# Issuing the transfers of v and of the weights from GpSimd's queue in an attention and gated-convolution kernel

## The chip, the cores and the metric

One core of a Trainium2 chip runs the program. The metric is the device time of one execution in microseconds (us), taken as the median of three runs. Engines are named as in the profile: PE (TensorE, with PEld for its weight loads), DVE (VectorE), ACT (ScalarE), POOL (GpSimd) and SP (SyncE). SPq is SP's queue, in which it issues transfers. Lnnn is a line of the kernel.

## The reference

Attention with a soft cap over 8 batches, 12 heads, 448 positions and a head size of 64, in float32, and behind it a gated feed-forward block:

```
scores = cap * tanh((q @ k.T / sqrt(64)) / cap)
attn   = exp(scores - max);  attn = attn / (sum(attn) + 1e-9)
x      = attn @ v, heads side by side      # (8, 448, 768)
gate   = sigmoid(conv over 5 positions of x with conv_w)
out    = (gate * (x @ w_val)) @ w_out
```

w_val and w_out are 768 x 768. They reach the kernel as 64-bit floats, and the kernel takes each apart into a high and a low part of 32 bits.

## The kernel before

Two heads of a batch make a pair; there are 48 pairs, and two pairs make a quad. For each pair the kernel loads q and k (`load_blocks`, L364: four transfers each, 56 KB apiece, in runs of 128 bytes), turns them by a transpose on DVE (`turn`, L515), multiplies q with k on PE (L542, and L553 for the remainder of 64 positions), and takes tanh and exp on ACT (L558, L562). Column sums (L610, into the tile `psz`) and the product with v (L636, into `psa` and `psz`) follow on PE, then a division and a convolution on DVE (L690), the product with w_val (L706 to L708), the gate, and the product with w_out (L741 to L743). The result goes out through `store` (ACT copies) and `store_out` (L754, a transfer from SP).

`load_v` brings v of a pair in three transfers: two of the tile `vn` (L377, 96 KB each) and one of `vh` (L378). `vn` and `vh` have two buffers each, and both pairs of a quad are read by all of its products with v, so that v of the next quad is loaded when these products have ended.

The weights come in twelve pieces, n = 0 to 5 of w_val and 6 to 11 of w_out, of 768 KB each. `weight_load(n)` (L451) brings piece n into `w_raw`, of which there is one buffer. Its conversion has three steps. The first reads `w_raw`: on DVE for pieces 0 to 3 (L306 to L309), on ACT for pieces 4 to 11 (L311, L312). The second is on DVE (L315, L316); L316 is the last to read `w_raw`, so piece n+1 can be loaded when L316 of piece n has ended. The third (L319 to L323, DVE) needs a copy of the piece that begins two bytes further on. For pieces 4 to 11 that copy is a second transfer of the same piece (`late_load`, L462, into the single buffer `w_late`), issued when the third step of the piece before has ended.

The tile `qkn` of q and k has one buffer through the first sixteen pairs, so q and k of a pair are loaded after `turn` of the pair before.

The order of the instructions on each engine is fixed: tables (PAIR, QUAD, BATCH, ONCE) give each step a due time in units of one pair, all steps are sorted by it, and each engine gets its instructions in that order. Every engine then works through its own list, and an instruction that waits holds up all that stand behind it on its queue. Before the change nearly all transfers stand in SP's list; ACT issues four at the very start, and POOL's list holds only seven memsets.

Of the kernel before, what the change touches and what calls it, by code (L numbers as in the profile page):

```python
# [20 lines left out]
P = 128  # L21
# [306 lines left out]
def quad_rows(w, g):  # L328

    return w[g * 2 * P:(g + 1) * 2 * P].rearrange("(p t) n -> p t n", t=2)  # L330
# [39 lines left out]
def load_v(nc, vn, vh, v, p):  # L370

    _, H, S, D = v.shape
    b, hp = divmod(p, H // 2)
    n = S // P * P
    r = p % 2 * (S - n)
    for j in range(2):
        nc.sync.dma_start(vn[:, j], v[b, 2 * hp + j, :n].rearrange("(t r) d -> r t d", r=P))  # L377
    nc.sync.dma_start(vh[r:r + S - n], v[b, 2 * hp:2 * hp + 2, n:].rearrange("j r d -> r j d"))  # L378


def fast_path(tc, io, u0, q, k, v, w_val, conv_w, w_out, out, capt):

    nc = tc.nc
    B, H, S, D = q.shape
# [14 lines left out]
    with ExitStack() as ctx:  # L399
# [48 lines left out]
        def weight_load(n):  # L448
            w, g, nh, _ = wsteps[n]
            wraw[n] = wsc.tile([P, 2, NH, 2], I32, name="w_raw")  # L450
            nc.sync.dma_start(  # L451
                wraw[n].rearrange("p t n two -> p t (n two)"), quad_rows(w.bitcast(I32), g)[:, :, nh * DM:(nh + 1) * DM]
            )

        def late_tile():
            return wsc.tile([P, 2, 4 * NH + 2], U16, name="w_late")

        def late_load(n):
            if n in BY_DMA:
                w, g, nh, _ = wsteps[n]  # L460
                wlate[n] = late_tile()
                nc.sync.dma_start(  # L462
                    wlate[n][:, :, 1:1 + 4 * NH], quad_rows(w.bitcast(U16), g)[:, :, nh * 2 * DM:(nh + 1) * 2 * DM]
                )

# [40 lines left out]
        def load_vp(p):  # L506
            if p % 2 == 0:
                vhalf[p // 2] = io.tile([P, 2, D], F32, name="vh")
            vloads[p] = io.tile([P, 2, NT, D], F32, name="vn")
            load_v(nc, vloads[p], vhalf[p // 2], v, p)  # L510
# [258 lines left out]
        def put(table, steps, count, unit, col):  # L769
# [16 lines left out]
        ), B, NPAIR, batch_column)  # L786
        steps = dict(
            weight_load=weight_load, late_load=late_load, val_first=val_first, weight_first=weight_first, weight_second=weight_second, weight_third=weight_third,
            free_scratch=free_scratch, free_pre=free_pre, cw_load=cw_load, cw_split=cw_split,
        )  # L790
# [179 lines left out]
```

## Time and profile before

| | |
|---|---|
| median of three runs | 689.23 us (688.55 to 689.86) |
| span of the profiled execution, first to last instruction | 686.2 us |
| PE busy | 659.0 us (96%) |
| DVE busy | 557.2 us (81%) |
| ACT busy | 499.7 us (73%) |
| POOL busy | 0.4 us |
| mean granted clock of TensorE | 0.992 |
| transfers issued by SP for v | 96 of `vn`, 48 of `vh` |
| transfers issued by SP for weights | 12 of `w_raw`, 8 of `w_late` |

No total time of the profiled execution is shown beside its span; the median of the runs stands 3.0 us above the span. A share of busy time is a mean over stages: the kernel first fills its pipeline and converts the weights, and then repeats one pattern for most of its time.

### The profile page before, as it was taken

How to read it: one execution, taken by the hardware profiler on the slowest of the kernel's cores; microseconds unless marked ns; L12 is line 12 of the kernel's file. 1: busy time of each engine (PE TensorE's matmuls, PEld its weight loads, DVE VectorE, ACT ScalarE, POOL GpSimd, SP SyncE). 2: the span in 40 equal slices, each digit the busy share in tenths (PEclk: the TensorE clock that was granted, in tenths of full speed). 3: DMA queues.
4: the chain of work that ended last, by engine and by line, in shares of the span. 5: the costliest groups of instructions: out<-in, count | busy, mean ns of one | idle time of the engine just before them, and what ended most of it. 6: DMA issues, size and time to landing. Idle time of an engine off the chain costs nothing.

```text
span 686.2 us, 11781 instructions
## 1 busy us (share of the span) xinstructions
PE 659.0 (96%) x4680; PEld 465.9 (68%) x4680; DVE 557.2 (81%) x776; ACT 499.7 (73%) x535; POOL 0.4 (0%) x7
## 2 busy tenths in 40 slices
PE   4787999999999999999999999999999999999996
PEld 1221484487596686786686696866766877767996
DVE  3899999989978889987979877988879896897530
ACT  5589769889684898777797695886788785975110
POOL 0000000000000000000000000000000000000000
PEclk9899999999999999999999999999999999999999
DMA  6769888423343432341334430433234432111001
GB/s 115 167 162 219 226 224 237 95 64 62 81 90 68 91 68 60 69 99 20 68 78 91 100 68 17 104 62 64 52 60 109 86 76 37 50 39 60 0 25 72
DMA packets 235165, 60.65 MB, mean 88 GB/s; under 512 B 226400, under 2 KB 226400, under 8 KB 235104
## 3 DMA queue, kind: packets, MB, share of 16 engines
q1 hardware_dynamic: 233248, 59.61, 39.2%
q8 instruction: 38, 0.62, 0.4%
q10 hardware_dynamic: 1856, 0.23, 0.3%
q14 instruction: 23, 0.19, 0.1%
HBM read 48.79 MB, written 11.01 MB: 87 GB/s over the span
## 4 chain that ended last, share of the span: by engine, by line
PE 86%; DVE 6%; SPq 3%; DMA 2%; issue 1%; ACT 1%; DVEq 0%; ACTq 0%
PE pss L542 13%; PE psa L636 10%; PE pss L706 9%; PE pss L708 8%; PE pss L707 8%; PE pss L741 8%; PE psz L636 8%; PE pss L743 7%; PE pss L742 7%; PE psz L610 4%; PE pss L553 3%; SPq L364 2%; DVE qkt L515 1%; DVE gate L690 1%; DMA qkn<-in_k_dram 1%
## 5 line engine op out<-in xcount | busy, mean ns | idle before, releaser
L558 ACT ACTIVATE pt<-pss,rc 128x896 f32<-128x896 f32 x144 | 139.8, 1003 | 69.6 <-PE pss L542 44.3
L562 ACT ACTIVATE pt<-pt,capt 128x896 f32<-128x896 f32 x144 | 145.5, 1041 | 0.6
L690 DVE SCALAR_TENSOR_TENSOR gate<-u,cw,gate 128x448 f32<-128x448 f32 x192 | 125.9, 674 | 1.7
L741 PE MATMUL pss<-wo,g_h 128*128 128x384 f32 x336 | 114.9, 342 | 0.0
L743 PE MATMUL pss<-wo,g_l 128*128 128x384 f32 x336 | 113.8, 339 | 0.0
L742 PE MATMUL pss<-wo,g_h 128*128 128x384 f32 x336 | 113.6, 338 | 0.0
L706 PE MATMUL pss<-xh,wv 128*128 128x448 f32 x288 | 105.8, 367 | 0.0
L707 PE MATMUL pss<-xh,wv 128*128 128x448 f32 x288 | 104.3, 362 | 0.0
L708 PE MATMUL pss<-xl,wv 128*128 128x448 f32 x288 | 104.3, 362 | 0.0
L741 PEld LDWEIGHTS pss<-wo,g_h 128*128 128x128 f32 x336 | 63.1, 188 | 9.3 <-ACT pt L558 5.7
L636 PE MATMUL psa<-pt,vn 128*32 128x448 f32 x576 | 69.1, 547 | 0.0
L636 PE MATMUL psz<-pt,vn 128*32 128x448 f32 x576 | 64.9, 541 | 0.7 <-DVE zt L641 0.7
L750 ACT COPY osb<-pss 128x768 f32<-128x768 f32 x28 | 22.3, 797 | 57.8 <-PE pss L743 56.8
L743 PEld LDWEIGHTS pss<-wo,g_l 128*128 128x128 f32 x336 | 63.1, 188 | 0.6 <-DVE g_l L425 0.6
L742 PEld LDWEIGHTS pss<-wo,g_h 128*128 128x128 f32 x336 | 63.1, 188 | 0.3 <-DVE wo L323 0.3
L706 PEld LDWEIGHTS pss<-xh,wv 128*128 128x128 f32 x288 | 54.0, 187 | 13.0 <-ACT pt L558 5.3
L515 DVE STREAM_TRANSPOSE qkt<-qkn 128x896 f32<-128x896 f32 x47 | 51.6, 1103 | 7.0 <-DMA qkn<-in_k_dram 3.5
L708 PEld LDWEIGHTS pss<-xl,wv 128*128 128x128 f32 x288 | 54.0, 188 | 3.6
L707 PEld LDWEIGHTS pss<-xh,wv 128*128 128x128 f32 x288 | 54.0, 188 | 3.5
L542 PE MATMUL pss<-qkt 64*128 64x448 f32 x144 | 37.5, 636 | 19.4 <-DVE guard L434 8.1
L586 DVE TENSOR_TENSOR pa<-pt 128x896 f32<-128x896 f32 x42 | 45.3, 1078 | 8.1 <-ACT pt L562 8.1
L718 DVE TENSOR_TENSOR gate<-pss,gate 128x896 f32<-128x896 f32 x24 | 26.1, 1088 | 31.1 <-PE pss L708 31.1
(86 smaller groups left out, 930.6 us busy)
## 6 DMA issues: line engine op xcount, KB each, us to landing
out_dram<-osb SPq DMA_DIRECT2D x28, 384.0 KB, 2.6
qkn<-in_q_dram SPq DMA_DIRECT2D x188, 56.0 KB, 2.3
qkn<-in_k_dram SPq DMA_DIRECT2D x188, 56.0 KB, 2.3
vn<-in_v_dram SPq DMA_DIRECT2D x96, 96.0 KB, 2.5
w_raw<-in_moe_w_val_dram SPq DMA_DIRECT2D x6, 768.0 KB, 4.8
w_raw<-in_moe_w_out_dram SPq DMA_DIRECT2D x6, 768.0 KB, 4.9
w_late<-in_moe_w_out_dram SPq DMA_DIRECT2D x6, 768.0 KB, 5.0
vh<-in_v_dram SPq DMA_DIRECT2D x48, 32.0 KB, 2.3
```

Source lines behind the costliest of these rows:

```text
L515: nc.vector.transpose(t.rearrange("p j s -> p (j s)"), loads.pop(p).rearrange("p j s -> p (j s)"))
L542: nc.tensor.matmul(ps[:, j, :S], st[x][r, 1, c], st[y][r, 0], start=(n == 0), stop=(n == len(parts) - 1))
L558: nc.scalar.activation(st["p", i], st.pop(("s", i)), AF.Tanh, scale=rc8)
L562: nc.scalar.activation(t, t, AF.Exp, scale=capt)
L636: nc.tensor.matmul(o, w, x, start=(q["n", t] == 1), stop=(q["n", t] == NT + 1))
L690: nc.vector.scalar_tensor_tensor(g, u, cw[:, i, c:c + 1], g, ALU.mult, ALU.add)
L706: nc.tensor.matmul(o[:, t, :S], w_h, xh, start=(c == 0), stop=False)
L707: nc.tensor.matmul(o[:, t, :S], w_l, xh, start=False, stop=False)
L708: nc.tensor.matmul(o[:, t, :S], w_h, xl, start=False, stop=(c == NCC - 1))
L741: nc.tensor.matmul(o[:, nh, :NH], g_h[:, d, s], w_h, start=(d == 0), stop=False)
L742: nc.tensor.matmul(o[:, nh, :NH], g_h[:, d, s], w_l, start=False, stop=False)
L743: nc.tensor.matmul(o[:, nh, :NH], g_l[:, d, s], w_h, start=False, stop=(d == NCC - 1))
```

## The change

144 transfers of v and 20 of the weights are issued from GpSimd's queue instead of SyncE's. The due times stay, so the moved transfers keep their order among themselves, and those that stay on SP keep theirs. Transfers of q, k, the convolution's weights and the output are as before, as are all buffers and all compute instructions.

```
@@ load_v
     for j in range(2):
-        nc.sync.dma_start(vn[:, j], v[b, 2 * hp + j, :n].rearrange("(t r) d -> r t d", r=P))
-    nc.sync.dma_start(vh[r:r + S - n], v[b, 2 * hp:2 * hp + 2, n:].rearrange("j r d -> r j d"))
+        nc.gpsimd.dma_start(vn[:, j], v[b, 2 * hp + j, :n].rearrange("(t r) d -> r t d", r=P))
+    nc.gpsimd.dma_start(vh[r:r + S - n], v[b, 2 * hp:2 * hp + 2, n:].rearrange("j r d -> r j d"))
@@ weight_load
-            nc.sync.dma_start(
+            nc.gpsimd.dma_start(
                 wraw[n].rearrange("p t n two -> p t (n two)"), quad_rows(w.bitcast(I32), g)[:, :, nh * DM:(nh + 1) * DM]
             )
@@ late_load
-                nc.sync.dma_start(
+                nc.gpsimd.dma_start(
                     wlate[n][:, :, 1:1 + 4 * NH], quad_rows(w.bitcast(U16), g)[:, :, nh * 2 * DM:(nh + 1) * 2 * DM]
                 )
```

## Rows read from the trace of the kernel before

**Rows 1.** The page's first part: busy time (share of the span) and instructions.

```profile
PE 659.0 (96%) x4680; PEld 465.9 (68%) x4680; DVE 557.2 (81%) x776; ACT 499.7 (73%) x535; POOL 0.4 (0%) x7
```

**Rows 2.** Busy time in stretches: PE, PEld, DVE, ACT, POOL, clock, DMA share, GB/s.

```profile
20.00:25.00 5.00, 3.36 (x12) 1.34 (x16) 4.23 (x13) 3.55 (x6) 0.00 (x0) 0.50 1.00 266
...
100.00:120.00 20.00, 20.00 (x149) 8.94 (x146) 18.87 (x27) 17.86 (x20) 0.00 (x0) 1.00 0.88 240
...
400.00:450.00 50.00, 50.00 (x347) 38.97 (x349) 40.95 (x55) 37.63 (x42) 0.00 (x0) 1.00 0.27 56
```

**Rows 3.** Waits of the compute engines, 78 to 140 us: total, times, longest.

```profile
PEld pss L742 <- DVE wo L323: 0.3, 1, 0.3
```

**Rows 4.** PE's timeline: start, length, instruction, idle before it and its releaser.

```profile
21.64 3.36 PE L542 MATMUL pss<-qkt 64*128 64x448 f32 x8 [5.48 <-DVE cw_m L306]
...
122.19 0.45 PE L742 MATMUL pss<-wo,g_h 128*128 128x384 f32 x1
```

**Rows 5.** DVE's timeline, the first 30 us.

```profile
10.99 1.11 DVE L515 STREAM_TRANSPOSE qkt<-qkn 128x896 f32<-128x896 f32 x1 [2.90 <-DMA qkn<-in_k_dram]
14.62 0.96 DVE L306 COPY w_late<-w_raw 128x1536 uint16<-128x1536 uint16 x1 [2.52 <-DMA w_raw<-in_moe_w_val_dram]
...
20.39 1.10 DVE L515 STREAM_TRANSPOSE qkt<-qkn 128x896 f32<-128x896 f32 x1
...
28.92 0.65 DVE L641 STREAM_TRANSPOSE zt<-psz 128x448 f32<-128x448 f32 x1 [1.69 <-PE psz L610]
```

**Rows 6.** SP's timeline, the first 20 us.

```profile
9.34 0.67 SPq L451 DMA_DIRECT2D w_raw<-in_moe_w_val_dram  x1
...
12.89 3.01 SPq L364 DMA_DIRECT2D qkn<-in_q_dram  x4
```

**Rows 7.** The chain that ended last, in order of time: start, length, what.

```profile
17.51 2.23 DMA qkn<-in_k_dram
```

**Rows 8.** ACT's timeline, conversion of the pieces 4, 8 and 9.

```profile
52.47 1.63 ACT L311 ACTIVATE w_t<-w_raw 128x768 f32<-128x768 f32 x1 [4.14 <-DMA w_raw<-in_moe_w_val_dram]
...
92.42 0.94 ACT L312 ACTIVATE w_raw<-w_raw 128x768 f32<-128x768 f32 x1
...
100.74 0.97 ACT L312 ACTIVATE w_raw<-w_raw 128x768 f32<-128x768 f32 x1
```

**Rows 9.** DVE's timeline, conversion of the pieces 4, 5, 8, 9 and 10.

```profile
55.52 0.96 DVE L316 TENSOR_TENSOR wv<-w_t,w_raw 128x768 fp32r<-128x768 f32 x1 [0.67 <-ACT w_raw L312]
...
69.17 0.56 DVE L319 TENSOR_SCALAR w_late<-w_late 128x768 int32<-128x768 int32 x1
...
93.53 0.96 DVE L316 TENSOR_TENSOR wo<-w_t,w_raw 128x768 fp32r<-128x768 f32 x1
...
101.77 0.96 DVE L316 TENSOR_TENSOR wo<-w_t,w_raw 128x768 fp32r<-128x768 f32 x1
...
110.70 0.96 DVE L316 TENSOR_TENSOR wo<-w_t,w_raw 128x768 fp32r<-128x768 f32 x1 [0.40 <-ACT w_raw L312]
```

**Rows 10.** SP's timeline, 60 to 90 us.

```profile
61.55 0.58 SPq L462 DMA_DIRECT2D w_late<-in_moe_w_val_dram  x1
...
80.74 0.55 SPq L462 DMA_DIRECT2D w_late<-in_moe_w_out_dram  x1
...
86.71 0.57 SPq L451 DMA_DIRECT2D w_raw<-in_moe_w_out_dram  x1
```

**Rows 11.** The tile w_raw: from issue to landing, shortest, median, longest.

```profile
DMA to landing us min/median/max: 4.6/4.9/5.9
```

**Rows 12.** The tile w_late: the same.

```profile
DMA to landing us min/median/max: 4.6/5.2/6.2
```

**Rows 13.** Issues of the tiles vn and qkn: ns shortest/median/longest, first and last start.

```profile
L377 SPq DMA_DIRECT2D vn<-in_v_dram x96: 368/487/1390, 19.1 to 624.0; - x96
...
L364 SPq DMA_DIRECT2D qkn<-in_q_dram x188: 311/477/1892, 5.3 to 567.9; - x188
```

**Rows 14.** Waits of SP's queue over the whole span: total, times, longest.

```profile
SPq L377 <- PE psa L636: 53.1, 4, 20.7
```

## Prediction

> **What bounds the kernel now.** I read the page's busy times first: PE works for 659.0 of a span of 686.2 us [rows 1], so about 27 us are all that any change of the queues could win. The view by stretches says where they lie. From some 80 us on PE is busy without a gap: 20.00 of 20 us at 100 to 120, 50.00 of 50 at 400 to 450, at full clock [rows 2]. In this long part a transfer that is issued earlier wins nothing, because PE has no gap to close. The gaps are at the start, where PE waits once for 5.48 us, and the clock stands at 0.50 (its lower level, 1.2 GHz) behind that gap, from 20 to 25 us [rows 2, 4].
>
> The second thing to see is that another engine stands just behind PE until the weights are converted. DVE is busy for 18.87 of the 20 us from 100 to 120 [rows 2], and at 122.19 us the product with w_out has to wait for DVE's last conversion step [rows 3, 4]. The wait is only 0.3 us, but it says that the conversion of the weights has no slack at its end. After it PE runs without gaps to the end, so whatever moves that point moves the end by as much. Thus the start must be followed along DVE, from the first turn to the last piece of w_out.
>
> Third I read, along this DVE line, which steps wait for a transfer. Each piece is loaded when L316 of the piece before has ended, is changed by ACT for nearly 2 us, and then comes back to DVE. In the pieces 8 and 9 ACT's L312 ends at 93.36 and 101.71, and DVE's L316 starts at 93.53 and 101.77 [rows 8, 9]: gaps of 0.17 and 0.06 us. In pieces 4 and 10 DVE already waits for ACT, by 0.67 and 0.40 us [rows 9], and in piece 4 ACT has waited 4.14 us for the transfer [rows 8]. The other late pieces (6, 7, 11) have wider gaps, and piece 5 waits on its second copy instead. So the latency of the w_raw transfer, median 4.9 us [rows 11], stands on the path in four of twelve pieces.
>
> **The change part by part.** The change takes 164 issues from SP and gives them to POOL, which has nothing else to do [rows 1]. Three effects follow.
>
> *a) The first piece is loaded earlier (gain).* On SP it is issued at 9.34, behind q and k of pair 1 [rows 6]; on DVE its conversion waits 2.52 us for it, until 14.62, though the turn of pair 1 has ended at 12.10 [rows 5]. POOL can issue it some 4 us earlier. Then DVE could convert from 12.10 on, and, at the 5.77 us that it takes (14.62 to 20.39), reach the turn of pair 2 at 17.9. That turn also needs k of pair 2, whose last transfer lands at 17.51 + 2.23 = 19.74 [rows 7]. Its loads start on SP at 12.89 and can start 0.71 us earlier without the issue of w_raw; the four of q took 3.01 us, where four medians make 1.9 [rows 6, 13], so up to 1.1 more if that came from the weight's transfer. k would land at 17.9 to 19.0, and the turn starts 1.4 to 2.5 us earlier. Against that, the weight's transfer now runs beside q and k of pair 1, and the first turn may slip. I take a gain of 1.3 us, with ends 0 and 2.5. It carries on, since PE's gap before 21.64 ends with this turn and DVE's next idle time, 1.69 us, is a wait for PE [rows 4, 5].
>
> *b) The same transfers from POOL take longer (loss).* The trace holds no transfer issued from POOL. Let c be the time that POOL's queue needs for one, where SP needs 0.49 for vn and 0.57 for w_raw [rows 10, 13]. From below it is bounded by SP's time; from above by the longest single issue in the trace, 1.89 us [rows 13]. I take twice SP's time of a weight, c = 1.1: nearer to the ordinary rows than to one outlier. Let what a landing takes longer be d = c - 0.55 = 0.55 us, if a transfer moves only once it is issued; the spread of the landings of w_raw, -0.3 to +1.0 about its median [rows 11], bounds d too. Then d falls on the path in pieces 4 and 10 in full (0.55 each), in piece 8 by 0.55 - 0.17 = 0.38, and in piece 9 by 0.55 - 0.06 = 0.49. Together 2.0 us. Pieces 1 to 3 and 5 to 7 and 11 hide it under DVE's other work; without that cover each would cost another 0.55.
>
> The Trainium skill (DMA: Bandwidth & Descriptors, Specifications) gives the first byte as about 1 us for GpSimd's path and 0.6 for SP's and ACT's; no run here shows it yet. By that figure d would be 0.4 (an estimate), this sum 0.4 + 0.4 + 0.23 + 0.34 = 1.4, and, with nothing under (c), the change would come out level.
>
> *c) POOL's queue falls behind where v stands ahead of a weight (loss).* The order of due times puts six transfers of v (two pairs) behind a transfer of weights and ahead of the next, at two places on the path. First: the second copy of piece 7 is issued at 80.74, six of v follow, and piece 8 at 86.71 [rows 10], when its buffer comes free. On POOL seven issues take 7.7 us, so that piece 8 leaves at 88.44: 1.7 us late, and piece 8 has no gap left under (b). Second: piece 5 is free to go when L316 of piece 4 ends, at 56.48 [rows 9]; with the six of v behind it POOL reaches the second copy of piece 5 at 56.48 + 7.7 = 64.2, where SP issued it at 61.55 [rows 10]. It lands 5.2 + 0.55 later [rows 12], at 69.9; DVE wants it at 69.17 [rows 9]. That is 0.8 us. Below c = 0.85 the first cost is nothing, below 1.0 the second.
>
> *d) q and k no longer stand behind v and the weights on SP (hidden).* v waits for its buffer on SP for up to 20.7 us at a time [rows 14], and what follows it waits too. This goes away, but those places lie in the part where PE has no gap [rows 2], and v on POOL has the whole time between the products of two quads. I cost it at nothing; the cover is PE's own work. The rule in the Trainium skill (DMA: Bandwidth & Descriptors, Issuing engines are not separate DMA queues) that issuing from several engines saves only the issue time agrees with the rows on PE.
>
> **The sum.** 2.0 + 1.7 + 0.8 - 1.3 = +3.2 us on the span, 686.2 to 689.4. The runs stand 3.0 us above the span, which I leave as it is: 689.23 + 3.2 = 692.4 us.
>
> **The rivals.**
>
> *Level.* If c is near 0.85, d is 0.3, (c) costs nothing and (b) is 0.3 + 0.13 + 0.24 + 0.3 = 1.0 us, against a gain of 1.3: 689 us. For it speaks that SP's issues are all near half a microsecond; against it that nothing in the trace ties POOL's time to SP's.
>
> *Faster.* The earlier turn of pair 2 shortens PE's gap before 21.64 so far that the clock does not fall. The eight matmuls there take 3.36 us at clock 0.50 [rows 2, 4]; at the full clock half, a gain of 1.7, and DVE's wait of 1.69 us for PE [rows 5] could use it. With POOL as quick as SP, 1.3 + 1.7 = 3.0 us: 686.2. This needs d below some 0.3 and a gap clearly shorter than 5.48 us. Against it: by my sum the gap still is over 4 us.
>
> *Much slower.* POOL's issues are held up by DVE, which is busy 18.87 of 20 us [rows 2], by one short conversion step of 0.56 us each time [rows 9]. Then c is some 1.6 and d about 1.0: (b) is 1.0 + 1.0 + 0.83 + 0.94 = 3.8, (c) 11.2 - 5.97 = 5.2 and 56.48 + 11.2 + 6.2 - 69.17 = 4.7, less 1.3: +12.4, 701.6 us. The Trainium skill (SBUF — State Buffer, Who interferes with whom) says that GpSimd, which builds the descriptors of its transfers itself, is locked out while DVE runs in a mode that uses two ports. No row of before can show it.
>
> *No change in effect* is not possible at c above 1: the path of the weights has no slack to hide it.
>
> **How the numbers follow.** A measurement of this kernel tells 0.2%, 1.4 us, from no change. c from about 1.0 to 1.4 gives +1.4 to +8 and is likeliest: 0.42. Much slower: 0.13. Level: 0.25. Faster by over 0.2%: 0.20. So slower 0.55, same 0.25, faster 0.20. The prediction is the first case, 692.4 us, its own range 690.7 to 697. The range for all: the low end, 687.5, lies inside the faster case; the high end, 702, takes in the centre of the much slower one.
>
> **What the profile of the changed kernel would show.** For (a), w_raw issued from POOL at about 5 us, no wait of DVE before L306, and the turn of pair 2 near 19. For (b), landings of w_raw well above 4.9 us, and DVE waiting for L312 in pieces 8 and 9 too. For (c), POOL's issues over 0.85 us apart, and piece 8 issued well after L316 of piece 7. At the meeting point, a wait of PE for L323 of about 3 us in place of 0.3. The prediction is wrong if POOL's issues take no longer than SP's, if landings don't grow, or if the clock stays up at 20 us.

## The result, and the profile after

The changed kernel takes 692.72 us (691.77 to 693.91, four runs) against 689.47 (688.55 to 689.86, four runs): a ratio of 1.0052, interval 1.0039 to 1.0065. It is slower by 3.3 us. The profiled execution took 693.91 us, 1.8 above its span of 692.1. Each timed run stands 1.8 to 1.9 us above its span, so the profiled execution of before was itself a quick one, about 1.2 us under the median of its three runs, where the prediction took that difference for a constant. The two traces therefore differ by more (5.9 us of span) than the medians.

The page's busy times answer to [rows 1]; under them are its lines on the queues of SP (q1) and POOL (q0): packets, MB, share of the 16 engines.

```profile
PE 663.7 (96%) x4680; PEld 467.2 (68%) x4680; DVE 558.6 (81%) x776; ACT 500.0 (72%) x535; POOL 118.4 (17%) x171
...
q1 hardware_dynamic: 182496, 32.86, 24.4%
q0 software_dynamic: 9024, 26.75, 12.6%
```

The instructions of PE, DVE and ACT are the same and stand in the same order; only the queues differ. The view by stretches answers to [rows 2]:

```profile
20.00:25.00 5.00, 2.98 (x8) 1.27 (x8) 3.82 (x11) 4.97 (x8) 3.69 (x6) 0.56 0.95 270
100.00:120.00 20.00, 19.22 (x143) 8.25 (x141) 18.00 (x27) 14.68 (x16) 2.90 (x4) 1.00 0.76 216
400.00:450.00 50.00, 50.00 (x338) 41.01 (x336) 41.34 (x54) 40.02 (x43) 7.92 (x12) 1.00 0.29 59
```

The long part is as full as before. At 100 to 120 PE now has gaps of 0.78 us, and DVE of 2.0 where it had 1.1: the loss lies in the start and the conversion. DVE's timeline there, first for [rows 5], then for pieces 8 and 10:

```profile
13.50 1.11 DVE L515 STREAM_TRANSPOSE qkt<-qkn 128x896 f32<-128x896 f32 x1 [5.36 <-DMA qkn<-in_k_dram]
14.54 0.92 DVE L306 COPY w_late<-w_raw 128x1536 uint16<-128x1536 uint16 x1
...
20.76 1.11 DVE L515 STREAM_TRANSPOSE qkt<-qkn 128x896 f32<-128x896 f32 x1 [0.39 <-DMA qkn<-in_k_dram]
...
29.75 0.65 DVE L641 STREAM_TRANSPOSE zt<-psz 128x448 f32<-128x448 f32 x1 [2.00 <-PE psz L610]
...
96.76 0.56 DVE L315 TENSOR_SCALAR w_t<-w_t 128x768 int32<-128x768 int32 x1 [0.44 <-ACT w_t L311]
97.71 0.96 DVE L316 TENSOR_TENSOR wo<-w_t,w_raw 128x768 fp32r<-128x768 f32 x1 [0.38 <-ACT w_raw L312]
...
117.77 0.56 DVE L319 TENSOR_SCALAR w_late<-w_late 128x768 int32<-128x768 int32 x1 [0.88 <-DMA w_late<-in_moe_w_out_dram]
```

The first piece is there when DVE wants it, so L306 waits no more, but it starts at 14.54 instead of 14.62: the wait has moved to the turn before, which k of pair 1 now holds up until 13.50 (10.99 before). From there the lag of the trace behind that of before can be read step by step: 0.37 us at the turn of pair 2, 0.83 at 29.75 (PE's low clock), 1.32 at L316 of piece 3, 1.60 at L316 of piece 4, 1.91 at the turn at 64.60, 3.19 at L641 at 75.58 (PE's clock again, 0.58 at 64 to 70 against 0.74), 4.18 behind piece 8, 5.17 behind the second copy of piece 10. The last copy of the output on ACT ends 5.0 us later; the remaining 0.9 lies behind it. What PE waits for at the meeting point has hardly grown, against [rows 3]:

```profile
PEld pss L742 <- DVE wo L323: 0.5, 1, 0.5
...
PE pss L742 <- DVE wo L323: 0.2, 1, 0.2
```

The landings, against medians of 4.9 and 5.2 in [rows 11, 12]:

```profile
w_raw<-in_moe_w_val_dram POOLq DMA_DIRECT2D x6, 768.0 KB, 5.4
w_raw<-in_moe_w_out_dram POOLq DMA_DIRECT2D x6, 768.0 KB, 5.4
w_late<-in_moe_w_out_dram POOLq DMA_DIRECT2D x6, 768.0 KB, 5.3
```

And POOL's own timeline at the place of term (c), where the prediction saw piece 8 held up behind six transfers of v:

```profile
84.24 0.72 POOL L462 DMA_DIRECT2D w_late<-in_moe_w_out_dram  x1 [1.65 <-DVE wo L323]
84.96 1.52 POOL L377 DMA_DIRECT2D vn<-in_v_dram  x2
86.48 0.61 POOL L378 DMA_DIRECT2D vh<-in_v_dram  x1
87.08 1.56 POOL L377 DMA_DIRECT2D vn<-in_v_dram  x2
88.64 0.61 POOL L378 DMA_DIRECT2D vh<-in_v_dram  x1
90.34 0.73 POOL L451 DMA_DIRECT2D w_raw<-in_moe_w_out_dram  x1 [1.10 <-DVE wo L316]
```

An issue takes 0.61 to 0.78 us, the queue is idle for 1.10 us before piece 8, and that piece leaves 0.29 us after its buffer came free (90.05). There is no backlog.

### The profile page after: what moved, and what is told of

Its sections match the earlier page's. It is cut to its first block, busy times and chain, and to the rows that moved or that the text cites. A ratio compares the mean times of both kernels' runs of the same rounds, so it can differ in the third digit from the quotient of the medians.

```text
span 692.1 us, 11846 instructions
## 1 busy us (share of the span) xinstructions
PE 663.7 (96%) x4680; PEld 467.2 (68%) x4680; DVE 558.6 (81%) x776; ACT 500.0 (72%) x535; POOL 118.4 (17%) x171
## 4 chain that ended last, share of the span: by engine, by line
PE 75%; DVE 5%; ACT 1%; issue 1%; DVEq 0%; ACTq 0%
PE pss L542 10%; PE psa L636 9%; PE pss L706 8%; PE pss L741 7%; PE pss L707 7%; PE pss L708 7%; PE pss L743 7%; PE pss L742 7%; PE psz L636 6%; PE psz L610 3%; PE pss L553 2%; DVE gate L690 1%; DVE pa L586 1%; ACT pt L558 1%; DVE qkt L515 1%; DVE pa L589 1%
## 5 line engine op out<-in xcount | busy, mean ns | idle before, releaser
L558 ACT ACTIVATE pt<-pss,rc 128x896 f32<-128x896 f32 x144 | 140.2, 1004 | 69.6 <-PE pss L542 44.7
L377 POOL DMA_DIRECT2D vn<-in_v_dram x96 | 73.4, 767 | 414.0 <-PE psz L636 287.3
```

What stands on the lines that cost most here:

```text
L377: nc.gpsimd.dma_start(vn[:, j], v[b, 2 * hp + j, :n].rearrange("(t r) d -> r t d", r=P))
L558: nc.scalar.activation(st["p", i], st.pop(("s", i)), AF.Tanh, scale=rc8)
```

## The experiments

The theory after this reading: two queues have no order between them, so a big transfer runs beside what stood ahead of it, and delays it; on top, each transfer from POOL comes a few tenths later. The rivals: later transfers by themselves (the prediction's (b)), or a disturbance that lasts through the whole kernel. The kernel before was timed again beside each set.

**Which part costs.** Four kernels undo a part of the change.

v alone on POOL:

```
@@ weight_load, late_load (after)
-            nc.gpsimd.dma_start(
+            nc.sync.dma_start(
```

> Only v's 144 transfers are issued from POOL; the weights and their second copies stay on SP. Theory 1 (the whole loss is in the weights: the first piece collides with q and k of pair 1, and later pieces land later): level with before, within 0.7 us, and turn of pair 2 still at 20.4. Theory 2 (POOL's issues of v slow DVE's steps that run beside them): a loss of 0.5 to 1.5 us, with DVE's L319 and L320 at 0.68 to 0.71 us where they overlap v's issues, instead of 0.55. Rival (v in the way on SP did cost something): faster by up to 1 us.

690.54 us, ratio 1.0024 (1.0015 to 1.0032). The size is that of theory 2, but its sign is not there: no L319 or L320 of this trace takes longer than 0.57 us. What the trace shows is another thing. Before, v of pairs 6 and 7 stood on SP behind the second copy of piece 7; now it leaves POOL when its buffers are free, at 78.16 to 82.6, while piece 7 is issued on SP at 79.31. That piece lands 6.4 us after its issue instead of 5.0. It is used 6.51 us after its release instead of 5.14, and ACT and DVE wait, which they did not before. First ACT's line of before, then the lines of this run:

```profile
83.32 0.91 ACT L311 ACTIVATE w_t<-w_raw 128x768 f32<-128x768 f32 x1
```

```profile
85.80 0.91 ACT L311 ACTIVATE w_t<-w_raw 128x768 f32<-128x768 f32 x1 [1.51 <-DMA w_raw<-in_moe_w_out_dram]
86.74 0.56 DVE L315 TENSOR_SCALAR w_t<-w_t 128x768 int32<-128x768 int32 x1 [0.46 <-ACT w_t L311]
87.69 0.97 DVE L316 TENSOR_TENSOR wo<-w_t,w_raw 128x768 fp32r<-128x768 f32 x1 [0.39 <-ACT w_raw L312]
```

The weights alone on POOL:

```
@@ load_v (after)
-        nc.gpsimd.dma_start(vn[:, j], ...
-    nc.gpsimd.dma_start(vh[r:r + S - n], ...
+        nc.sync.dma_start(vn[:, j], ...
+    nc.sync.dma_start(vh[r:r + S - n], ...
```

> Only the 12 loads of w_raw and the 8 of w_late are issued from POOL; v stays on SP. Theory 1: nearly the whole loss, +2.5 to +3.5 us against before. Theory 2: less, +1.5 to +2.5, since DVE's steps at 42 to 48 and 60 to 63 us keep their lengths. Rival (the loss is v's alone): level.

693.67 us, 1.0060 (1.0045 to 1.0075). The weights alone lose as much as the whole change, some 4 us and more than theory 1 expected. The two halves add up to 0.84%, more than the whole change's 0.52%. That fits the theory, by which v and the weights stand in one queue again when both are on POOL; it is no proof of it, with intervals of about 0.1 to 0.15% either way.

The first piece back on SP:

```
@@ weight_load (after)
-            nc.gpsimd.dma_start(
+            (nc.gpsimd if n else nc.sync).dma_start(
```

> As the changed kernel, but piece 0 of the weights is issued from SP as before, behind q and k of pair 1. If the collision with q and k of pair 1 is a cost that carries through: turn of pair 1 at 11.0 instead of 13.5, DVE 0.8 us earlier at 30 us, and a time 0.8 to 2.1 us below the changed kernel (690.6 to 691.9), the upper part if the clock stands higher at 65 to 70 us. Rival (later waits absorb it): no change, 692.7.

692.36 us, 1.0052 (1.0038 to 1.0067): no different from the whole change. The turn of pair 1 is back at 10.91, but the time does not follow. The two intervals together leave room for a gain of about 1 us, so this run only shows that the collision at the start is no large part; piece 0 moved alone (below) agrees.

The second copies back on SP:

```
@@ late_load (after)
-                nc.gpsimd.dma_start(
+                nc.sync.dma_start(
```

> As the changed kernel, but the eight second copies are issued from SP. If the wait of 0.88 us for the second copy of piece 10 counts, and the loads of w_raw land sooner without a second copy beside them in the same queue: 0.9 to 1.5 us below the changed kernel, 691.2 to 691.8. Rival (the copy then stands behind q and k on SP, and DVE waits as long): no change.

692.11 us, 1.0054 (1.0035 to 1.0073). No gain is seen, so the second copies are not the main cause. The intervals do not exclude the lower end of the 0.9 to 1.5 us that were expected.

**The suspected costs by themselves.** This kernel computes nothing of the reference and writes zeros. It times one weight piece at a time from SP, then from POOL; q and k of a pair alone, and with a piece ahead of, behind and beside them; and conversion steps of DVE beside issues of v.

```
            for i in range(6):
                weight(w_pool, nc.gpsimd)
                nc.vector.tensor_copy(acc, w_pool[:, 1, 767:768])
                nc.vector.tensor_copy(acc, w_pool[:, 0, 0:1])
            for t, queue, first in ((qk_a, None, True), (qk_b, nc.sync, True), (qk_b, nc.sync, False), (qk_c, nc.gpsimd, True), (qk_c, nc.gpsimd, True)):
...
            for tiles, halves, queue in ((vs, vhs, nc.sync), (vp, vhp, nc.gpsimd)):
...
                steps(12)
```

> No part of the reference is computed and the output is filled with zeros: only the disputed transfers and DVE steps run, each by itself. Phase 1: a 768 KB piece of w_val six times from SP, then six times from POOL, each load waiting for DVE's read of the one before. Theory 1 (POOL's path itself is slower): 0.4 to 0.8 us more from POOL per load. Rival (the path is as fast, the landings grow by company on the DMA engines): within 0.3 us. Phase 2: q and k of one pair (eight transfers) alone, then with a weight piece ahead of them from SP, then with the piece behind them from SP, then with the piece from POOL at the same time. If company decides: the eight need some 2 us more with the piece from POOL than alone, about as much as with the piece ahead in the same queue, and next to nothing more with the piece behind them. Phase 3: 12 times a one-input step and a two-input step on DVE alone, beside 18 transfers of v from SP, beside the same from POOL. If POOL's issues take a port of DVE: the one-input step grows from 0.56 to about 0.70 us beside POOL, and stays beside SP; the two-input step stays.

A piece costs 5.3 us from one issue to the next on SP and 5.6 on POOL: 0.1 is a longer landing, 0.3 a later issue, since POOL issues 0.3 us after what it waited for has ended (0.03 on SP). From the first issue to the second transpose, q and k take 5.9 us alone, 6.0 with the piece behind them, 8.2 with it ahead, and 7.6 and 7.8 with it on POOL beside them. SP's timeline shows the four issues of k alone and beside the piece:

```profile
68.41 2.04 SPq L55 DMA_DIRECT2D qk_a<-in_k_dram  x4
...
93.20 3.81 SPq L55 DMA_DIRECT2D qk_c<-in_k_dram  x4
```

So a piece in another queue costs q and k 1.6 to 1.8 us, nearly as much as one ahead of them in their own (2.3). DVE's steps with one input, 0.55 us alone (0.64 beside SP's transfers, at the same pace of 1.34 us a pair of steps), take 0.70 to 0.72 in three of the ten cases beside POOL's issues and 0.56 to 0.64 in the others; those with two stay at 0.94 there after the first:

```profile
142.90 0.70 DVE L98 TENSOR_SCALAR step<-step 128x768 int32<-128x768 int32 x1
143.52 0.94 DVE L99 TENSOR_TENSOR two<-two 128x768 f32<-128x768 f32 x1
...
145.76 0.56 DVE L98 TENSOR_SCALAR step<-step 128x768 int32<-128x768 int32 x1
```

Twelve pairs of steps take 16.66 us beside eighteen transfers of v from POOL, 16.06 beside SP's.

**One part alone, from the kernel before.** Six kernels move one part of the transfers each.

```
@@ load_v: v of pairs 6 and 7 only; v of the pairs from 8 on only
+        (nc.gpsimd if p in (6, 7) else nc.sync).dma_start(vn[:, j], ...
+        (nc.gpsimd if p >= 8 else nc.sync).dma_start(vn[:, j], ...
@@ weight_load: w_raw of the pieces 8 to 11; 4 to 7; the first piece
+            (nc.gpsimd if n >= 8 else nc.sync).dma_start(
+            (nc.gpsimd if 4 <= n <= 7 else nc.sync).dma_start(
+            (nc.sync if n else nc.gpsimd).dma_start(
@@ load: k of pair 1 only
+                load_blocks(nc, loads[p][:, j], src, p, nc.scalar if p == 1 and j else None)
```

> The kernel before, but v of pairs 6 and 7 alone (six transfers) is issued from POOL. Theory (v overtakes: on its own queue it leaves as soon as its buffers are free, beside the load of piece 7, instead of behind the second copy of piece 7): L311 of piece 7 waits 1 us or more, and the time rises by 0.8 to 1.5 us, most of what moving all of v costs. Rival (the loss comes from the many issues of v in the later part): level, within 0.4 us.

689.77 us, 1.0011 (1.0002 to 1.0020). That is some 0.8 us, the lower end of the theory's range, but less than half of v's 0.24%, where the theory had most of it; the interval alone does not exclude the rival's 0.4 us. The trace shows the overtaking: piece 7 lands 5.8 us after its issue (5.0 before), and ACT waits for it:

```profile
84.08 0.90 ACT L311 ACTIVATE w_t<-w_raw 128x768 f32<-128x768 f32 x1 [0.92 <-DMA w_raw<-in_moe_w_out_dram]
```

> Only v of the pairs 8 to 47 goes out from POOL: 120 of the change's 164 transfers, all in the part where PE has no gap; everything up to pair 7 stays on SP. Theory (the loss is made in the start and conversion stage alone, by company and by later landings): 0.0 us, within 0.6 us of the kernel before, and POOL's waits for psz and psa take the place of SP's. Rival (SP and POOL disturb the steady part too, by DVE's steps beside POOL's issues or by q and k): a steady part longer by 0.15 us per quad, 20 quads, so +1.5 to +3 us.

688.82 us, 0.9993 (0.9983 to 1.0002). Level: 120 of the 164 moved transfers cost nothing and bring nothing, as term (d) had it. The loss of v lies in the pairs before; the share that pairs 6 and 7 leave was not followed further.

> The kernel before, but w_raw of pieces 8 to 11 is issued from POOL; v, the second copies and pieces 0 to 7 stay on SP. By my recorded step (each piece lands later by d on a path without slack, with d now 0.3 us of later issue plus up to 0.5 of landing): +1 to +2.5 us. Rival (POOL's path is no slower and nothing overtakes here): +0.3 to +1.0, the later issue alone on three pieces.

689.89 us, 1.0011 (1.0003 to 1.0020). In its trace DVE waits 0.38 us in piece 8, 0.41 in piece 9, and 0.82 and 0.39 in piece 10, where before it waited 0.20 and 0.40. These three pieces leave POOL 0.3 us after their release and land 0.2 to 0.4 us later than before. Each is later, as the recorded step has it, but the time rises by 0.8 us, below that step's range and inside the rival's.

> Only w_raw of the pieces 4 to 7 goes out from POOL; the second copies, the other pieces and v stay on SP. Theory (each weight from POOL starts 0.3 us after its release and lands 0.1 to 0.5 us later; pieces 4 and 6 have ACT waiting for them, 5 and 7 have slack): DVE's L316 of piece 4 waits 0.4 to 0.8 us longer than the 0.67 of before, pieces 5 and 7 cost nothing, +0.4 to +0.8 us at the meeting point and +0.3 to +1.0 in the time. Rival (a weight loses its place among q, k and v, so that the pieces where PE's low clock also falls lose more): piece 4 or 6 is used 1.5 us or more later after its release than before, and the time rises by 1.5 to 3 us, most of what the weights alone lost.

691.15 us, 1.0030 (1.0017 to 1.0044), and half of the weights' 0.60%. My theory's 0.3 to 1.0 us was too small; what the rival foresaw came for piece 4, used 6.69 us after its release (4.93 before):

```profile
55.15 0.56 DVE L315 TENSOR_SCALAR w_t<-w_t 128x768 int32<-128x768 int32 x1 [1.26 <-ACT w_t L311]
56.52 0.96 DVE L316 TENSOR_TENSOR wv<-w_t,w_raw 128x768 fp32r<-128x768 f32 x1 [0.81 <-ACT w_raw L312]
```

The piece left POOL at 47.18, its second copy SP at 49.92. What each queue moved at 51.5 to 53 shows the end of its load:

```profile
q1 hardware_dynamic: 120, 0.37, 83.9%
q0 software_dynamic: 10, 0.02, 4.6%
```

The piece's last ten packets go out in 1.5 us while the second copy, issued 2.7 us later, takes the engines. That looks like company again, here between two parts of one piece, but this is not shown: piece 4 landed after 4.7 to 4.8 us in all eight traces in which it came from SP, and from POOL after 6.0 to 6.3 in four traces and 4.8 in the changed kernel's; in two of those four its second copy stood in the same queue. Why it lands late there stays open.

> Only piece 0 of w_val goes out from POOL, at about 5.3 us. The prediction's term (a): k of pair 2 lands 1.4 to 2.5 us earlier, the turn of pair 2 starts near 18 to 19 instead of 20.4, and the time falls by 1.3 us. Theory (the piece runs beside q and k of pair 1 and holds them up, since no queue puts k first any more): turn of pair 1 near 13.5 instead of 11.0, L306 without a wait at 14.5, turn of pair 2 at 20.4 to 20.8, and the time within -0.3 to +0.5 us.

688.46 us, 0.9995 (0.9986 to 1.0003): level, not the 1.3 us of term (a). k's four issues take 3.60 us instead of 2.04, the turn of pair 1 comes at 12.62, L306 without a wait at 13.65, the turn of pair 2 at 19.66, 0.73 earlier. By L323 of the last piece the trace is 1.11 us late: PE's low clock at 64 to 70 us (0.59 against 0.74) and a wait of 0.91 us for the second copy of piece 10 came in between, and a gain this small drowns in them. Level is what the theory foresaw, though both turns come earlier than it said.

> The kernel before, but the four transfers of k of pair 1 are issued from ACT, which waits at that time. If the start is bound by SP's issues: SP reaches piece 0 and q of pair 2 some 1.9 us earlier, the turn of pair 1 starts 1 us earlier or more, DVE's wait for piece 0 shrinks, and the time falls by 1 to 2 us. Rival (the DMA engines, not SP's issues, set the landing there): level.

692.49 us, 1.0046 (1.0027 to 1.0066). This one tells nothing of queues side by side: the four issues stand behind L558 in ACT's list, leave at 11.35, and the turn of pair 1 starts at 15.90. It does show that a lag at the start, 2.25 us at L323 of piece 0, is not absorbed later: the time rises by 3.1.

**A version that is faster than both.** If order is what counts, k must go out ahead of the piece. POOL's queue is empty at 5.2 us:

```
@@ load (before)
-                load_blocks(nc, loads[p][:, j], src, p)
+                load_blocks(nc, loads[p][:, j], src, p, nc.gpsimd if p == 1 and j else None)
```

> The first piece earlier without a change of who is served first: k of pair 1 goes out from POOL's empty queue at 5.3 us beside q on SP, and piece 0 follows q on SP at 7.25 instead of 9.34. Nothing else moves. Theory (order decides: k stands ahead of the piece in time, all four k by about 8.3): turn of pair 1 at 11 to 12.5, L306 of piece 0 at 12.5 to 13.8 instead of 14.6, turn of pair 2 0.4 to 1.8 us earlier, and the time 0 to 1.5 us shorter. Rival (any two queues at once slow each other as much as they save): the last two issues of k share the engines with the piece, turn of pair 1 near 13 to 13.5, turn of pair 2 unchanged or later, time -0.2 to +1.

687.35 us (686.03 to 688.71), 0.9978 (0.9968 to 0.9989): faster than before by 0.22%, 1.5 us, and, by the two ratios, than the change by 0.7%. Its timelines of SP, POOL and DVE:

```profile
5.28 1.89 SPq L364 DMA_DIRECT2D qkn<-in_q_dram  x4
7.21 0.68 SPq L451 DMA_DIRECT2D w_raw<-in_moe_w_val_dram  x1
```

```profile
5.25 2.61 POOL L364 DMA_DIRECT2D qkn<-in_k_dram  x4 [0.45 <-issue]
```

```profile
11.01 1.11 DVE L515 STREAM_TRANSPOSE qkt<-qkn 128x896 f32<-128x896 f32 x1 [2.93 <-DMA qkn<-in_k_dram]
12.95 0.96 DVE L306 COPY w_late<-w_raw 128x1536 uint16<-128x1536 uint16 x1 [0.82 <-DMA w_raw<-in_moe_w_val_dram]
...
18.76 1.10 DVE L515 STREAM_TRANSPOSE qkt<-qkn 128x896 f32<-128x896 f32 x1
```

The turn of pair 1 is where it was, the piece comes 1.67 us earlier, the turn of pair 2 1.63, and 1.11 of it is left at L323 of the last piece. This is the gain that term (a) hoped for. One thing is not parted here: in POOL's queue k moves in 128 packets (0.23 MB, some 1.75 KB each) instead of packets of 128 bytes, so the size of its packets changed along with the order.

## Why the prediction was right, and where it was not

The direction was right, but that the time came out so near, 692.4 against 692.72, is luck. Only one of the terms, (d), had the right size. Two wrong ones, of +2.5 and -1.3, stood in for costs that were not in the sum.

*(a), a gain of 1.3 us: failed.* The step that failed is that the piece's company was named ("the first turn may slip") and not priced. While the piece moves, k nearly stops. SP's issues of k in the trace of before, and in the changed one:

```profile
7.25 2.04 SPq L364 DMA_DIRECT2D qkn<-in_k_dram  x4
```

```profile
7.33 4.36 SPq L364 DMA_DIRECT2D qkn<-in_k_dram  x4
```

The queues from 8 to 9.5 us, before and changed:

```profile
q1 hardware_dynamic: 1359, 0.17, 70.0%
```

```profile
q0 software_dynamic: 81, 0.50, 87.1%
q1 hardware_dynamic: 74, 0.01, 4.0%
```

Before, k moves 1359 packets in these 1.5 us. Beside the piece it moves 74, nearly as many as the piece (81), but its own hold 128 bytes and the piece's 6 KB. The Trainium skill (DMA: Bandwidth & Descriptors, Queues, rings and completion order) says that each engine takes the queues that have work in turn, a packet at a time; this stretch agrees, 81 to 74 as the profile counts packets. Not every stretch does: the end of piece 4 above has 10 packets of one queue beside 120 of the other. Alone the move of piece 0 gave -0.05% (-0.14 to +0.03) instead of -0.19%. Nor was the 1.69 us DVE's next idle time in the trace of before: two waits of 0.30 us stand ahead of it, for ACT at 21.86 and for piece 1 at 23.31.

*(b), 2.0 us from later landings in pieces 4, 8, 9 and 10: in part right.* The transfers do land later and DVE does wait for them, and the landing's median grew by 0.5 us as taken (d = 0.55). But its reason does not carry that size: by the prediction's own d = c - 0.55, the measured c of 0.72 gives 0.17. A piece alone lands only 0.1 us later from POOL; the rest comes beside other transfers. And 0.3 us of later issue, which the prediction did not have, came on top. Alone, pieces 8 to 11 cost 0.11% (0.8 us; the sum had 1.4 for them) and pieces 4 to 7 0.30% (2.1 us; it had 0.55). In the changed kernel's trace piece 4 costs 0.27 us, piece 8 0.82, pieces 9 and 10 next to nothing, and the second copy of piece 10, which had no term, 0.88. One reading was wrong without harm: in the trace of before DVE does not wait for the second copy of piece 5.

*(c), 2.5 us of backlog: failed.* It hung on c, mis-sized: 0.72 for a piece and 0.77 for vn instead of 1.1. Below 0.85 the text itself gave nothing, and nothing came.

*(d), nothing: right.* 0.9993 for v from pair 8 on.

*Not in the sum:* v overtaking a piece (0.11% for pairs 6 and 7 alone), and DVE's steps beside POOL's issues. In the changed kernel's trace four steps with one input that run beside issues of v are longer than before (0.56 us each), without any wait:

```profile
42.38 0.68 DVE L320 TENSOR_SCALAR w_t<-wv 128x768 int32<-128x768 int32 x1
...
60.30 0.70 DVE L319 TENSOR_SCALAR w_late<-w_late 128x768 int32<-128x768 int32 x1
60.92 0.71 DVE L320 TENSOR_SCALAR w_t<-wv 128x768 int32<-128x768 int32 x1
...
88.31 0.69 DVE L315 TENSOR_SCALAR w_t<-w_t 128x768 int32<-128x768 int32 x1
```

Together they cost some 0.6 us. L309 (1.06) and L315 (0.68) of piece 3, at 46.42 and 47.19, are longer too, but not for this reason: POOL's last issue of v before them ended at 44.07, and with the weights alone on POOL, where no issue stands beside them, they take 1.05 and 0.71. Some 0.2 of the lag at piece 3 is its landing, 5.8 us after the issue (4.8 before), just when DVE starts on it at 44.82.

The single parts add up to 0.30 + 0.11 + 0.11 - 0.05 - 0.07 = 0.40%, 2.8 us of the 0.52%. Two of these are level within their intervals; pieces 1 to 3, the second copies and v of the first six pairs were not tried alone; and as the two halves do not add up, the single parts need not either. So which transfers lose is shown in part, and the rest stays open.

*The rivals.* Level had the nearest c (0.85; measured 0.72 to 0.77), and missed because the loss does not come from c. Much slower had the right conflict with the roles turned round: POOL's issues are seldom longer than usual (vn 0.77 us on average, the longest weight 1.39), while DVE's steps beside them can be. The Trainium skill (SBUF — State Buffer, Who interferes with whom) says that whoever comes first holds the shared port; longer steps of DVE agree with that. That it is the port which makes them longer, no run here shows by itself. Faster fails at the clock: PE's gap before the products of pair 2 is 3.92 us instead of 5.48 [rows 4], and they still take 3.35 us at a granted clock near its lower level (0.56 at 20 to 25 us):

```profile
22.02 3.35 PE L542 MATMUL pss<-qkt 64*128 64x448 f32 x8 [3.92 <-DVE cw_m L306]
```

*The signs to look for.* None of the three signs of being wrong came: an issue from POOL takes 0.72 us against SP's 0.57 for a piece, landings grew from 4.9 to 5.4, and the clock fell at 20 us as before. The 3 us of wait at the meeting point did not come, and that sign was ill chosen: what PE does before that point depends on DVE too and moves with it, so the lag shows as many small gaps (19.22 of 20 us) and not as one wait.

The clock is the uncertain part of the traces. In each trace a stretch near the lower level (0.50 is 1.2 GHz) falls between 55 and 72 us, at another place each time (0.54 at 60 to 65 with the first piece on SP, 0.58 at 64 to 70 in the change), and moves a trace by about 1.3 us. Whether the change makes it longer on average, the runs do not settle: the mean granted clock is 0.988 over the change's four runs and 0.990 over the 17 of the kernel before that were timed beside the halves. But with the weights alone it is 0.991 over six runs, and they lose as much. So a lower clock is not needed for the loss.

## What to carry to other kernels

A queue is also an order: before a transfer is moved to another one, look up what stood ahead of it and behind it, because from then on it runs beside both, and here small packets lost to big ones. Try the free queue for what is wanted first, not for what is biggest: k of one pair from POOL gained 0.22% here, 164 transfers of weights and v lost 0.52%. When a stage has no slack, tenths of a microsecond per transfer count, so price the later issue, the landing beside company, and the steps of other engines that run beside the issues.

## What was not expected of the hardware

- From 8 to 9.5 us two queues shared the engines nearly packet for packet, whatever the packets held: 81 packets of 6 KB beside 74 of 128 bytes, and the issues of k on SP took 4.36 us instead of 2.04 meanwhile.
- POOL issues a transfer in 0.61 (vh), 0.72 (a piece) or 0.77 us (vn), and starts 0.3 us after its wait has ended; SP takes 0.5 to 0.6 and starts after 0.03.
- Some DVE steps with one input took 0.70 us instead of 0.55 beside POOL's issues (three of ten in the kernel of transfers alone); steps with two inputs did not grow.
